# Three edits to an attention and mixture-of-experts kernel: batch 1's late values by split products, the first expert in five chunks, 512-column products in the last two second layers

## The chip, the cores and the metric

The kernel runs on one core of one Trainium2 chip. The metric is the device time of one execution in microseconds (us); the time of a kernel is the median of its timed runs. A profile of one more execution shows where each engine's time goes.

## The reference

An attention over channels feeds a mixture of experts. Cut to what matters:

```python
# attention: B, N, C = 4, 5056, 256
qn = q / (norm(q, axis=1) + 1e-6);  kn = k / (norm(k, axis=1) + 1e-6)
a = softmax(kn.T @ qn / tau)            # 256 x 256 for each batch
x = (v @ a).reshape(20224, 256)         # the "values"
# experts: E = 8, F = 1024, cap = 20224 / 8 = 2528
logits = x @ w_gate
# all (token, expert) pairs in order of falling logit: a token goes to the first
# expert that still has room; each expert ends with 2528 tokens
out[mask_e] = relu(x[mask_e] @ w1[e]) @ w2[e]
```

## The kernel before

**Values.** Each batch has five chunks (b, c) of 1024 rows, the last one padded, and a chunk has eight tiles of 128 rows (t). A tile of values is v times a, a contraction over 256 channels in two halves (kb). It can be made in two ways. `x_tiles` (L260) multiplies in plain float32: two matmuls of 256 columns, which the trace shows as four. `x_tiles_cut` (L572) works with float32r numbers: v and a are each held as a high and a low half, and a tile takes six matmuls of 256 columns: high·high, high·low and low·high for each kb. This is called a tile by three products. `cleave` (L559) makes the halves of half a chunk (four tiles): ScalarE writes minus the high half, an accumulating DMA issued by GpSimd adds v from DRAM to it, which leaves the low half, and ScalarE writes the high half. Batch 0 is made by three products while the scores are still being computed (L306), batch 2 by `x_tiles_cut`, batches 1 and 3 in plain float32.

**Routing.** When all logits are there, `route` (L615) finds each expert's members one expert after another: eight rounds each of a VectorE comparison (`ge`, L728), a TensorE count (`pc`, L693), small VectorE reductions and a second small product (L706). Then `compact` and `listed` write the list of the expert's rows (`src`, L1014). For expert 0 the list comes in two parts: the first four columns of 128 rows (`HEAD` = 4, taken from the rows stored so far) and the other sixteen. The routing of expert p + 1 runs while expert p is computed.

**The order around the change.** The tail of the values is an order written out by hand: `TURNS` is a string of F and C. F makes half a chunk of the `PLAIN` list (two pairs of tiles) in plain float32, C half a chunk of the `CLOVEN` list by three products. Meanwhile VectorE routes expert 0. After the last turn the kernel waits, in its planned time, for the first list; then it makes the last eight pairs of tiles (`LATE` = 8), which are batch 3's chunks 3 and 4. In front of the last of these pairs `turn_both` transposes chunk 0 of expert 0, which has two columns. A planner (`Order`, L1106) holds estimated clocks of TensorE (`o.pe`) and VectorE (`o.dve`). While the main work is written down, it places the routing's steps in each engine's order when the planned clock has passed their readiness. The engines themselves keep that order and wait on semaphores.

**Experts.** An expert's 20 columns are cut into chunks: `FIRST_CUT` = 2, 4, 4, 4, 4, 2 for expert 0, `CUT` = 4, 4, 4, 4, 4 for the others. `load_x` gathers the rows of a chunk by one indirect DMA for each column. They are transposed by TensorE (`turn`, L1423; the first three chunks of expert 0 and chunks that are in a hurry) or by VectorE and DMAs (`stage`), and split into `xH` and `xL`. `layer1` (L1480) makes eight blocks `ph` of 128 hidden units with six products each; ScalarE writes `hH`, VectorE `hL`. `layer2` (L1523) makes for each column a `py` of 256 outputs in 24 products: for each of eight blocks hH·wH, hH·wL and hL·wH. ScalarE copies `py` to `y`, and GpSimd scatters the rows. Layers of neighbouring chunks are interleaved: layer 1 of chunk c, then layer 2 of chunk c − 1. `split_piece` (L1244) splits the weights in quarters. For expert 0, what of them is not split by the start of its first layer is split right there, before it.

Of the kernel before, what the change touches and what calls it, by code (L numbers as in the profile page):

```python
# [8 lines left out]
F32 = mybir.dt.float32  # L9
# [60 lines left out]
PLAIN = ((3, 0), (1, 2), (3, 1), (3, 2), (1, 3), (1, 4), (3, 3), (3, 4))  # L70
CLOVEN = ((2, 4), (2, 0), (2, 1), (2, 2), (2, 3))
TURNS = "FFCFCFCFCFCFCFCFCFFCFC"
PLACES = ("ub0", "ub1", "ua0", "ua1", "ub0", "ub1", "vr", "ua0", "ua1", "ua2")
BEHIND = {3: "FF", 4: "C", 5: "CC", 6: "FFFF", 7: "CCC", 8: "CCCC", 9: "FFFFFF"}
FREED = (9, 10)
CUT = (4, 4, 4, 4, 4)
FIRST_CUT = (2, 4, 4, 4, 4, 2)
# [21 lines left out]
DEPTH = 3  # L99
WOVEN = range(1, E - 1)  # L100
# [4 lines left out]
def attention_moe(ctx: ExitStack, tc: tile.TileContext, q, k, vt, tau, wg, w1t, w2t, tabs, out):  # L105
# [21 lines left out]
    ps_2 = Banks("s0", "s1")  # L127
# [428 lines left out]
    cloven = [(b, c, h) for b, c in CLOVEN for h in range(0, T, TH)]  # L556
    v_cut = []

    def cleave():  # L559
        b, c, h = cloven[len(v_cut)]  # L560
        home = PLACES[len(v_cut)]
        y = (vp.tile([128, 2048], F32, name="vr", bufs=BUFS_V) if home == "vr" else
             ffw.tile([128, 2048], F32, name=home)).bitcast(F32R)
        y = y.rearrange("p (z k n) -> p z k n", z=2, k=2)
        raw = vs[b, c][:, :, h:h + TH].rearrange("p k t n -> p k (t n)")
        S.activation(y[:, 1], raw, AF.Copy, scale=-1.0)
        P.dma_start(out=y[:, 1], in_=vt[b, c].rearrange("p (k n) -> p k n", k=2)[:, :, h * 128:(h + TH) * 128],
                    accum_op=OP.add)
        S.activation(y[:, 0], raw, AF.Copy)
        v_cut.append(y.rearrange("p z k (t n) -> p z k t n", t=TH))  # L570

    def x_tiles_cut(k, t, xs, tick):  # L572
        b = cloven[k][0]
# [640 lines left out]
    cuts = [FIRST_CUT] + [CUT] * (E - 1)  # L1214
# [28 lines left out]

    def split_piece(p, i, q_, eng):  # L1244
# [6 lines left out]
        if i == 1:  # L1251
# [49 lines left out]
    phs = []  # L1301
    turned = [0]
# [154 lines left out]
    def turn_both():  # L1457
        xg = xgs[0, 0]
        ready[0, 0] = 2
        nt = n_of(0, 0)  # L1460
        xH, xL = xts[0, 0] = (ffx.tile([128, 2, 512], F32R, name="xH"), ffx.tile([128, 2, 512], F32R, name="xL"))
        pt = ps_t.tile([128, 512], F32, name="pt")
        for i in range(cuts[0][0]):
            for kb in range(2):
                PE.transpose(pt[:, kb * nt + i * 128:kb * nt + (i + 1) * 128].bitcast(F32R),
                             xg[:, i, kb * 128:(kb + 1) * 128].bitcast(F32R), identr)
        for kb in range(2):
            rows, hi = even_odd(pt[:, kb * nt:(kb + 1) * nt]), in_turn(xH, kb, nt)
            S.activation(hi, rows, AF.Copy)
            V.tensor_tensor(in_turn(xL, kb, nt), rows, hi.bitcast(F32), op=OP.subtract)  # L1470
        o.pe += 450
        o.dve = max(o.dve, o.pe + 1200)

# [49 lines left out]
    def layer2(p, c, h, inserts):  # L1523
# [4 lines left out]
        wH, wL = wt[p, 1]  # L1528
        o.until(("out", p))
        settle()  # L1530
        pace_2 = 2 if p < 2 else 3
        for i, col in enumerate(cols_of(p, c)):
# [5 lines left out]
            py = ps_2.tile([128, 512], F32, name="py")  # L1538
            j = 0
            for fb in range(8):  # L1540
                for l, w in ((hH, wH), (hH, wL), (hL, wH)):
                    w = w.rearrange("p (g a f m) -> p g f m a", g=4, a=2, f=2)[:, fb // 2, fb % 2]
                    PE.matmul(py[:n, 0:C], lhsT=l[:, fb, tk], rhs=w, start=(j == 0), stop=(j == 23))  # L1543
                    j += 1
                    if j == 12:
                        for fn in inserts.get((i, j), ()):
                            fn()
                        advance(2, i * 2688 + 1344, (2, p, c))
                    if j % pace_2 == 0:
                        o.tick(pace_2 * 112)  # L1550
            y = ffx.tile([128, C], F32, name="y", bufs=4)
            S.activation(y[:n], py[:n, 0:C], AF.Copy)  # L1552
            P.memset(spacer[:, 0:1], 0.0)
# [226 lines left out]
```

## Time and profile before

| | |
|---|---|
| timed runs | 1222.14, 1218.46, 1221.15 us; median 1221.15 us |
| the profiled execution | 1213.0 us, of which the span is 1211.1 us |
| TensorE busy | 1195.4 us (99%) |
| VectorE busy | 863.6 us (71%) |
| ScalarE busy | 580.8 us (48%) |
| GpSimd busy | 407.8 us (34%) |
| mean granted clock of TensorE | 0.999 |

The span is the time from the first to the last event of the profile; the execution's own time is a little longer. The busy times of one engine never overlap with themselves, so an engine at 99% leaves 1% of the span in which it did nothing. Shares are means over stages that differ.

### The profile page before, as it was taken

How to read it: one execution, taken by the hardware profiler on the slowest of the kernel's cores; microseconds unless marked ns; L12 is line 12 of the kernel's file. 1: busy time of each engine (PE TensorE's matmuls, PEld its weight loads, DVE VectorE, ACT ScalarE, POOL GpSimd, SP SyncE). 2: the span in 40 equal slices, each digit the busy share in tenths (PEclk: the TensorE clock that was granted, in tenths of full speed). 3: DMA queues.
4: the chain of work that ended last, by engine and by line, in shares of the span. 5: the costliest groups of instructions: out<-in, count | busy, mean ns of one | idle time of the engine just before them, and what ended most of it. 6: DMA issues, size and time to landing. Idle time of an engine off the chain costs nothing.

```text
span 1211.1 us, 23720 instructions
## 1 busy us (share of the span) xinstructions
PE 1195.4 (99%) x8885; PEld 1095.1 (90%) x8885; DVE 863.6 (71%) x2428; ACT 580.8 (48%) x1326; POOL 407.8 (34%) x655
## 2 busy tenths in 40 slices
PE   8999999999999999999999999999999999999997
PEld 6889977898998989899999999999999999999997
DVE  7788695778888888988887888887764444435330
ACT  6566654656434453444353464364465544344331
POOL 1000001111442552354425443443444345444422
PEclk9999999999999999999999999999999999999999
DMA  8999986785333132323422242243234233422310
GB/s 313 362 397 318 405 323 209 182 232 225 113 105 122 59 103 79 124 75 99 152 88 75 90 157 97 84 162 99 88 130 136 87 117 126 147 92 95 105 65 34
DMA packets 70546, 183.82 MB, mean 152 GB/s; under 512 B 11168, under 2 KB 34592, under 8 KB 65824
## 3 DMA queue, kind: packets, MB, share of 16 engines
q1 hardware_dynamic: 39808, 97.01, 22.3%
q0 software_dynamic: 20656, 63.72, 17.5%
q10 hardware_dynamic: 9968, 21.59, 4.7%
q8 instruction: 69, 1.13, 0.4%
q14 instruction: 45, 0.37, 0.1%
HBM read 122.77 MB, written 59.24 MB: 150 GB/s over the span
## 4 chain that ended last, share of the span: by engine, by line
PE 88%; DVE 4%; issue 4%; POOL 2%; DMA 1%; ACT 0%; POOLq 0%; SPq 0%; ACTq 0%; DVEq 0%
PE ph L1506 32%; PE py L1543 31%; PE s L343 9%; PE px L265 5%; PE pc L693 2%; PE px L306 2%; PE px L581 2%; PE px L459 1%; POOL out_dram L1554 1%; DMA ua<-in_q_dram 1%; DVE acc_k L353 1%; DVE acc_q L353 1%; PE pi L933 1%; PE pt L933 0%; DVE nf L410 0%
## 5 line engine op out<-in xcount | busy, mean ns | idle before, releaser
L1543 PE MATMUL py<-ua,hH 128*128 128x256 f32 (+1 forms) x2560 | 438.4, 277 | 0.0
L1506 PE MATMUL ph<-xH,ua 128*128 128x512 f32 (+3 forms) x1312 | 393.4, 375 | 0.3 <-DVE hL L1515 0.3
L1543 PEld LDWEIGHTS py<-ua,hH 128*128 128x128 f32 (+1 forms) x2560 | 389.3, 190 | 1.7
L1543 PE MATMUL py<-ua,hL 128*128 128x256 f32 (+1 forms) x1280 | 352.8, 276 | 0.0
L1515 DVE SCALAR_TENSOR_TENSOR hL<-ph,hH 128x512 fp32r<-128x512 f32 (+3 forms) x328 | 217.6, 666 | 111.1 <-ACT hH L1510 110.3
L1510 ACT ACTIVATE hH<-ph 128x512 fp32r<-128x512 f32 (+3 forms) x328 | 191.0, 583 | 198.2 <-PE ph L1506 196.8
L1506 PEld LDWEIGHTS ph<-xH,ua 128*128 128x128 f32 x1312 | 244.6, 189 | 30.1 <-DVE hL L1515 1.4
L1554 POOL DMA_INDIRECT out_dram<-y,idx x160 | 162.3, 1015 | 292.8 <-ACT y L1552 239.1
L1506 PE MATMUL ph<-xL,ua 128*128 128x512 f32 (+3 forms) x656 | 245.1, 374 | 0.0
L1543 PEld LDWEIGHTS py<-ua,hL 128*128 128x128 f32 (+1 forms) x1280 | 243.9, 191 | 0.0
L1276 POOL DMA_INDIRECT xg<-x_d,src x160 | 164.6, 1029 | 90.7 <-issue 51.5
L1552 ACT ACTIVATE y<-py 128x256 f32<-128x256 f32 (+1 forms) x160 | 61.5, 384 | 259.1 <-PE py L1543 199.9
L343 PE MATMUL s<-ua 128*128 128x256 f32 (+1 forms) x640 | 144.8, 385 | 5.7 <-DMA ua<-in_q_dram 5.7
L343 PEld LDWEIGHTS s<-ua 128*128 128x128 f32 (+1 forms) x640 | 121.7, 193 | 25.4 <-DMA ua<-in_q_dram 5.7
L1506 PEld LDWEIGHTS ph<-xL,ua 128*128 128x128 f32 x656 | 124.2, 189 | 13.9 <-DVE xL L1448 0.8
L352 ACT ACTIVATE sq<-ua 128x1024 f32<-128x1024 f32 (+1 forms) x80 | 76.8, 970 | 49.5 <-DVE acc_k L353 15.4
L1374 DVE TENSOR_TENSOR xL<-xT,xH 128x256 fp32r<-128x256 f32 (+1 forms) x136 | 50.3, 419 | 59.1 <-ACT xH L1370 59.0
L1287 POOL COPY spacer<-hH 1x1 f32<-1x1 f32 x110 | 25.9, 235 | 154.4 <-ACT hH L1510 144.7
L373 POOL TENSOR_SCALAR ny<-ny 128x4 f32<-128x4 f32 x4 | 2.0, 504 | 179.6 <-ACT ny L372 179.6
L1257 DVE TENSOR_TENSOR ua<-ub,ua 128x512 fp32r<-128x512 f32 x64 | 47.1, 745 | 14.8 <-ACT ua L1254 13.8
L1370 ACT ACTIVATE xH<-xT 128x256 fp32r<-128x256 f32 (+1 forms) x136 | 52.2, 448 | 2.6 <-DMA xT<-via 2.6
L353 DVE TENSOR_TENSOR acc_k<-acc_k,sq 128x1024 f32<-128x1024 f32 (+2 forms) x40 | 44.2, 1112 | 10.4 <-ACT sq L352 9.5
(346 smaller groups left out, 1419.8 us busy)
## 6 DMA issues: line engine op xcount, KB each, us to landing
x_d<-xs ACTq DMA_DIRECT2D x40, 512.0 KB, 5.4
ua<-in_k_dram SPq DMA_DIRECT2D x35, 512.0 KB, 6.5
ua<-in_q_dram SPq DMA_DIRECT2D x35, 512.0 KB, 7.5
via<-xs SPq DMA_DIRECT2D x33, 512.0 KB, 2.7
xT<-via SPq DMA_DIRECT2D x132, 128.0 KB, 2.8
vr<-in_vt_dram SPq DMA_DIRECT2D x14, 1024.0 KB, 10.3
ua<-in_vt_dram SPq DMA_DIRECT2D x4, 1024.0 KB, 4.8
ua<-in_vt_dram POOLq DMA_DIRECT2D x5, 512.0 KB
```

Of the source, the lines that this page charges most:

```text
L265: mm = PE.matmul(px[:, i * C:i * C + width], lhsT=vs[b, c][:, kb, t + i, :], rhs=a_f[b][:, kb, 0:width], start=(kb == 0), stop=(kb == 1))
L343: newest[0] = PE.matmul(sb[:, ib * C:(ib + 1) * C], lhsT=kt[:np_, t, ib * 128:(ib + 1) * 128], rhs=qt[:np_, t, :], start=(first and t == 0 ...
L352: S.activation(sq[:n, t0:t1], t_[:n, t0:t1], AF.Square)
L353: V.tensor_tensor(acc[:n, t0:t1], acc[:n, t0:t1], sq[:n, t0:t1], op=OP.add)
L1276: P.indirect_dma_start(out=xg[:n, i, :], out_offset=None, in_=rows, in_offset=bass.IndirectOffsetOnAxis(ap=routed[p]["src", col][:n, col:c ...
L1370: S.activation(hi[:, a], rows[:, a], AF.Copy)
L1506: PE.matmul(ph[:, 0:nt], lhsT=l[:, w], rhs=in_turn(x_, kb, nt).rearrange("p a m -> p m a"), start=(i == 0), stop=(i == 5))
L1510: S.activation(hH[:, fb, 0:nt], ph[:, 0:nt], AF.Relu)
L1515: V.scalar_tensor_tensor(hL[:, fb, 0:nt], ph[:, 0:nt], 0.0, hH[:, fb, 0:nt].bitcast(F32), op0=OP.max, op1=OP.subtract)
L1543: PE.matmul(py[:n, 0:C], lhsT=l[:, fb, tk], rhs=w, start=(j == 0), stop=(j == 23))
L1552: S.activation(y[:n], py[:n, 0:C], AF.Copy)
L1554: sd = P.indirect_dma_start(out=out, out_offset=bass.IndirectOffsetOnAxis(ap=routed[p]["idx", col][:n, col:col + 1], axis=0), in_=y[:n], i ...
```

## The change

1. Batch 1's chunks 2, 3 and 4 move from `PLAIN` to `CLOVEN`: six half chunks that were F become C. Their low halves come from a VectorE subtraction (v minus its high half), not from a DMA; a's halves for batch 1 are made by `halve_a_1`. `TURNS` has six F and sixteen C instead of twelve and ten. One more buffer, `own`, holds halves.
2. Expert 0 is cut like the others, in five chunks of four columns. Its first chunk is gathered in front of the last but one late pair and transposed by `turn`, one half in front of each of the last two pairs. Pieces of the weights left over are split between the blocks of its first layer. The second layer of a first chunk waits for the first part of the list alone.
3. In experts 6 and 7 (`WIDE` = 6) w2's halves lie side by side, and hH·wH and hH·wL become one product of 512 columns into the two halves of a PSUM bank. ScalarE copies the second half, VectorE adds the first, and four banks take turns. The last column of the last expert stays as it was.

```diff
+PLAIN = ((3, 0), (3, 1), (3, 2), (3, 3), (3, 4))
+CLOVEN = ((2, 4, 0), (1, 2, 0), (2, 4, 4), (1, 2, 4), (2, 0, 0), (1, 3, 0), (2, 0, 4), (1, 3, 4), (2, 1, 0), (1, 4, 0), (2, 1, 4),
+          (1, 4, 4), (2, 2, 0), (2, 2, 4), (2, 3, 0), (2, 3, 4))
-TURNS = "FFCFCFCFCFCFCFCFCFFCFC"
+TURNS = "FFCCCCFCCCCFCCCCFCCFCC"
+PLACES = ("ub0", "ub1", "own", "ua0") * 3 + ("vr", "vr", "vr", "own")
-FIRST_CUT = (2, 4, 4, 4, 4, 2)
+SUM_LAT = 700
+WIDE = 6
...
+    def halve_a_1():
+        a = a_f[1][:, :, 0:C].rearrange("p k (m a) -> p k m a", a=2)
+        less = x_rows()[:, 0:2].rearrange("p k (m a) -> p k m a", a=2)
+        h = apart(apool.tile([128, 2, GW], F32R, name="a0"))[:, :, :, 0:128]
+        S.activation(h.rearrange("p a k m -> p k m a"), a, AF.Copy)
+        V.tensor_tensor(less, a, h.rearrange("p a k m -> p k m a").bitcast(F32), op=OP.subtract)
+        lo = apart(apool.tile([128, 2, GW], F32R, name="a1"))[:, :, :, 0:128]
+        S.activation(lo.rearrange("p a k m -> p k m a"), less, AF.Copy)
...
+        if b == 2:
+            S.activation(y[:, 1], raw, AF.Copy, scale=-1.0)
+            P.dma_start(out=y[:, 1], in_=vt[b, c].rearrange("p (k n) -> p k n", k=2)[:, :, h * 128:(h + TH) * 128],
+                        accum_op=OP.add)
+            S.activation(y[:, 0], raw, AF.Copy)
+        else:
+            S.activation(y[:, 0], raw, AF.Copy)
+            unit[0] += 1
+            o.post(o.pe + TURN_LAT, 1120,
+                   lambda: V.tensor_tensor(y[:, 1], raw, y[:, 0].bitcast(F32), op=OP.subtract), unit[0])
+            lows_of[len(v_cut)] = unit[0]
...
+    cuts = [CUT] * E
...
-        o.until(("out", p))
+        o.until(("out", p, 0) if c == 0 else ("out", p))
...
+                todo = [(one, hH, wH), (one, hH, wL), (one, hL, wH)]
+                if twice:
+                    todo = [(py[:n], hH, w.rearrange("p a z m -> p (z m) a")), (one, hL, wH)]
...
-            S.activation(y[:n], py[:n, 0:C], AF.Copy)
+            S.activation(y[:n], py[:n, C:2 * C] if twice else one, AF.Copy)
+
+            def store(py=py, y=y, col=col, n=n, twice=twice):
+                if twice:
+                    V.tensor_tensor(y[:n], py[:n, 0:C], y[:n], op=OP.add)
...
-            if n == LATE - 1:
+            if n == LATE - 2:
                 queue[:] = head[:HEAD]
                 while queue:
                     gather()
-                turn_both()
+            if n >= LATE - 2:
+                turn(0, 0, n - LATE + 2)
             pair(*at_)
...
-        for i, q_, eng in cut_w[0][1:]:
-            split_piece(0, i, q_, eng)
...
-                h[0] = layer1(p, 0, {} if p == 0 else {2: [turn_at(1, 0)], 7: [turn_at(1, 1)], **pieces})
+                left_w = {2 * at: [lambda x=x: split_piece(0, *x)] for at, x in enumerate(cut_w[0][1:])}
+                h[0] = layer1(p, 0, left_w if p == 0 else {2: [turn_at(1, 0)], 7: [turn_at(1, 1)], **pieces})
...
-                    layer2(p, 0, h[0], {1: [turn_at(1, 0)], (1, 12): [turn_at(1, 1)]})
+                    layer2(p, 0, h[0], {3: [turn_at(1, 0)], (3, 12): [turn_at(1, 1)]})
```

## Rows read from the trace of the kernel before

**Rows 1.** The page: the span, then busy time, share and instructions of each engine.

```profile
span 1211.1 us, 23720 instructions
PE 1195.4 (99%) x8885; PEld 1095.1 (90%) x8885; DVE 863.6 (71%) x2428; ACT 580.8 (48%) x1326; POOL 407.8 (34%) x655
```

**Rows 2.** Windows: from:to, length, each engine's busy time (instructions), granted clock, DMA.

```profile
240.00:255.00 15.00, 15.00 (x149) 14.02 (x148) 12.13 (x39) 11.69 (x19) 3.26 (x3) 1.00 1.03 257
311.00:424.00 113.00, 112.39 (x958) 105.06 (x956) 96.02 (x312) 46.67 (x122) 48.35 (x75) 1.00 0.28 93
988.00:1100.00 112.00, 112.00 (x758) 105.27 (x757) 50.05 (x85) 46.32 (x94) 49.90 (x84) 1.00 0.38 123
```

**Rows 3.** The chain of waits in order of time: start, us, what.

```profile
225.20 2.68 PE px L581 x24
227.88 3.46 PE px L265 x16
...
984.60 10.36 PE ph L1506 x48
994.96 10.66 PE py L1543 x96
...
1015.98 10.72 PE py L1543 x96
```

**Rows 4.** Timeline of TensorE: start, us, operation, count, idle before it.

```profile
287.15 0.16 PE L913 MATMUL pc<-cb,before 128*128 128x1 bf16 x1 [0.67 <-DVE cb L907]
...
307.96 0.64 PE L1465 MATMUL pt<-identr,xg 128*128 128x128 f32 x4
...
330.01 0.28 PE L1442 MATMUL pt<-identr,xg 128*128 128x128 f32 x1 [0.31 <-DMA xg<-x_d,src]
...
432.59 0.45 PE L1442 MATMUL pt<-identr,xg 128*128 128x128 f32 x4
...
521.92 0.47 PE L1442 MATMUL pt<-identr,xg 128*128 128x128 f32 x4
```

**Rows 5.** Groups by line: busy us, mean ns of one, idle before.

```profile
L353 DVE TENSOR_TENSOR acc_k<-acc_k,sq 128x1024 f32<-128x1024 f32 (+2 forms) x40 | 44.2, 1112 | 10.4 <-ACT sq L352 9.5 <-ACT acc_k L348 0.5
...
L569 ACT ACTIVATE ua<-vr 128x1024 fp32r<-128x1024 f32 x5 | 5.2, 1040 | 0.0
```

**Rows 6.** Timeline of VectorE: expert 0's routing, and one addition of 256 columns.

```profile
219.28 0.82 DVE L609 TENSOR_TENSOR eq<-L 128x640 f32<-128x640 f32 x1
...
284.49 0.17 DVE L1014 COPY_PREDICATED src<-early,w__2663 128x4 int32<-128x4 int32 x1
...
306.53 0.18 DVE L1014 COPY_PREDICATED src<-early,w__2783 128x16 int32<-128x16 int32 x1
...
310.12 0.42 DVE L1470 TENSOR_TENSOR xL<-pt,xH 128x256 fp32r<-128x256 f32 x1 [0.45 <-ACT xH L1469]
```

**Rows 7.** DMA issues by line: count, KB each, median us from issue to landing.

```profile
xg<-x_d,src POOLq DMA_INDIRECT x160, 2.8
...
ub<-in_vt_dram POOLq DMA_DIRECT2D x4, 512.0 KB, 8.3
```

**Rows 8.** Timelines of ScalarE's queue and GpSimd: last store, gathers of three chunks.

```profile
297.19 0.33 ACTq L275 DMA_DIRECT2D x_d<-xs  x1
...
300.80 0.95 POOL L1276 DMA_INDIRECT xg<-x_d,src  x1 [20.90 <-ACT xs L269]
...
305.09 0.94 POOL L1276 DMA_INDIRECT xg<-x_d,src  x1 [0.30 <-issue]
...
424.70 0.97 POOL L1276 DMA_INDIRECT xg<-x_d,src  x1 [0.30 <-issue]
...
515.70 0.98 POOL L1276 DMA_INDIRECT xg<-x_d,src  x1 [0.16 <-issue]
```

**Rows 9.** List columns written (L1014), experts 1 and 2: count, durations, first and last start.

```profile
L1014 DVE COPY_PREDICATED src<-early,w__4187 x2: 170/174/179, 396.3 to 412.2; 128x6 int32<-128x6 int32 x1, 128x14 int32<-128x14 int32 x1
L1014 DVE COPY_PREDICATED src<-early,w__5817 x2: 171/175/179, 502.6 to 515.4; 128x6 int32<-128x6 int32 x1, 128x14 int32<-128x14 int32 x1
```

More of the change, by code (lines that the diff above doesn't have):

```diff
@@ L1250, in split_piece @@
         raw, h, lo = raw[:, sl], h[:, sl], lo[:, sl]
-        if i == 1:
+        if i == 1 and p >= WIDE:
+            raw = raw.rearrange("p (f m a) -> p f a m", f=2, a=2)
+            h, lo = (blocks(p, q_ * 2)[:, q_ % 2 * 2:q_ % 2 * 2 + 2, :, z] for z in range(2))
+        elif i == 1:
             raw = raw.rearrange("p (m a) -> p a m", a=2)
@@ L1455, in turn @@
             load_ahead(p, c)
[L1457 to L1472, printed above, removed]
     def load_ahead(p, c):
@@ L1544, in layer2 @@
                     j += 1
-                    if j == 12:
-                        for fn in inserts.get((i, j), ()):
+                    if fb == 3 and at_end:
+                        for fn in inserts.get((i, 12), ()):
                             fn()
                         advance(2, i * 2688 + 1344, (2, p, c))
-                    if j % pace_2 == 0:
+                    if twice:
+                        o.tick(218 if to is not one else 110)
+                    elif j % pace_2 == 0:
@@ L1550, in layer2 @@
                         o.tick(pace_2 * 112)
             y = ffx.tile([128, C], F32, name="y", bufs=4)
-            S.activation(y[:n], py[:n, 0:C], AF.Copy)
-            P.memset(spacer[:, 0:1], 0.0)
-            sd = P.indirect_dma_start(out=out, out_offset=bass.IndirectOffsetOnAxis(
-                ap=routed[p]["idx", col][:n, col:col + 1], axis=0),
-                                      in_=y[:n], in_offset=None)
-            for s_ in scat:
-                tc.declare_no_dep(sd.ins, s_.ins, reason="each token is written once")
@@ L1559, in layer2 @@
-            scat.append(sd)
+            S.activation(y[:n], py[:n, C:2 * C] if twice else one, AF.Copy)
+            def store(py=py, y=y, col=col, n=n, twice=twice):
+                if twice:
+                    V.tensor_tensor(y[:n], py[:n, 0:C], y[:n], op=OP.add)
+                P.memset(spacer[:, 0:1], 0.0)
+                sd = P.indirect_dma_start(out=out, out_offset=bass.IndirectOffsetOnAxis(
+                    ap=routed[p]["idx", col][:n, col:col + 1], axis=0),
+                                          in_=y[:n], in_offset=None)
+                for s_ in scat:
+                    tc.declare_no_dep(sd.ins, s_.ins, reason="each token is written once")
+                scat.append(sd)
@@ L1560, in layer2 @@
+            if twice:
+                unit[0] += 1
+                pys.append(unit[0])
+                o.post(o.pe + SUM_LAT, 400, store, unit[0])
+            else:
+                if p >= WIDE:
+                    o.flush(unit[0])
+                store()
             settle()
@@ L1570, in first_w @@
         def first_w():
+            assert past.count("C") >= 10
             load_w(0, 0)
@@ L1597, in attention_moe @@
         place()
+        halve_a_1()
         P.memset(ge[:, :, NT:J], 0.0)
         for kind in TURNS:
-            while len(v_cut) < len(cloven) and len(v_cut) <= len(past) + 1:
-                want_ = BEHIND.get(len(v_cut), "")
-                if any(past.count(x) < want_.count(x) for x in set(want_)):
-                    break
+            while len(v_cut) < len(CLOVEN) and len(v_cut) <= len(past) + 1 and len(v_cut) < past.count("C") + 4:
                 cleave()
@@ L1620, in attention_moe @@
         actx.close()
+        cctx.close()
         px_at[1] = False
```

52 lines of the change are left out of this document (31 added, 21 removed).

## The prediction

> **What bounds the kernel now.** I read the page first: the span is 1211.1 us and TensorE is busy for 1195.4 of them, VectorE for 863.6 [rows 1]. So all but 15.7 us of the span is matmul time, and the first question for each edit is how much TensorE time it takes away. The windows come second, because the share is a mean: while expert 0 is routed between the values, TensorE has no gap and VectorE is busy for 12.13 of 15 us; while expert 0 is computed VectorE is busy for 96.02 of 113 us, and from 988 to 1100 us, in the last experts, for 50.05 of 112 [rows 2]. The granted clock is 1.00 in all of them, so the 2.4 GHz level holds and no price here is one of a slow clock. VectorE therefore has room at the end of the kernel and little in front of it, and the second question is whether its new work makes a routing list late. The chain of waits gives the prices of products without idle time in between [rows 3]; the timelines show how close the lists and gathers come to the products that need them [rows 4, 6, 8, 9].
>
> **The change part by part.** All sums are in microseconds against the profiled execution, 1213.0 us around its span of 1211.1. The median of the runs shown is 1221.15, so 8.15 are added at the end; the last execution's extra time is taken as common to both kernels.
>
> *Values of batch 1.* Half a chunk in plain float32 takes 3.46 (16 instructions), by three products 2.68 (24 instructions) [rows 3]. The difference is 0.78; six half chunks save 4.68. They cost ScalarE six writes of a high half at 1.040 each, 6.2 in all [rows 5], which is hidden: ScalarE is busy for 11.69 of 15 us in its densest window, the four PSUM buffers of the values let it lag by some products, and batch 2's ten DMA halves are now spread over a longer stretch. They cost VectorE six subtractions of 1024 elements a row, at 1.112 like the additions of that size [rows 5], and one of 512 for a; by half of that row about 0.6, together 7.3. This work stands in front of or inside expert 0's routing, which runs on VectorE from 219.28 to the first list at 284.49 [rows 6]. VectorE is idle for a fifth of this stretch, but in short waits for TensorE's counts, so I take 5.5 of the 7.3 as delay; the bounds are 0 (all in the gaps) and 7.3. What is late next: the first list at 290.0 in place of 284.5. It is needed by the first gather, at 300.80, and that gather starts 3.6 after the last store issued at 297.19 [rows 8], so it waits for the store and not for the list. In the new kernel the stores end some 4.7 us earlier, so the gather would start near 296: still 6 us behind the list. Cost nothing, with 1 at most if the planner's clock runs ahead while it waits for the list.
>
> *Low halves of batch 2.* The order CCCC instead of FCFC shortens the lead of an accumulating DMA. It needs 8.3 from issue to landing [rows 7]. It is issued about one and a half C after the C that frees its place, and used after two or three more C, one F and a routing count: 2.68 × 2.5 + 3.46 = 10.2 from issue. Margin about 2; the row gives a median and no spread, so I allow 0 to 2 of stall and take 0.3.
>
> *Expert 0 in five chunks.* Columns stay the same. One chunk of 512 columns replaces two of 256: 48 products at 10.36 / 48 = 0.2158 instead of 96 at 10.72 / 96 = 0.1117 [rows 3], 0.36 less. TensorE transposes the first three chunks, now twelve columns instead of ten: four transposes more, below 0.45 for four [rows 4]. The two cancel. The wait of 0.31 for a gather at 330.01 [rows 4] should go, since chunk 2 is now needed a whole layer later, and the 0.67 of waiting at 287.15 may go, as the second list's count moves behind it among the late pairs: I take 0.6 for both together, from 0 to 0.98. Against that, the first chunk's transposes now need four gathered columns, and in front of the last but one pair. From the first gather at 300.80 the fourth was issued at 305.09 and lands 2.8 later, at 307.9 [rows 7, 8]. The transposes stood at 307.96 [rows 4], seven pairs of 1.73 (half of 3.46) behind the last turn, which so ended near 295.9; the fourth column landed 12.0 after that. In the new order the transposes follow after six pairs, 10.4. So the wait is 1.6 at most, and less by the second list's counts, which now fall among the late pairs and hold up the pairs but not the gathers; I take 0.4, with 0 below. The splitting of leftover weights stands in front of nothing that TensorE needs at once.
>
> *Products of 512 columns.* Per block the old form takes three products at 0.1117, 0.335; the new one takes 0.2158 + 0.1117 = 0.3275. That is 0.0075 less, for 8 blocks × 39 columns (two experts of 20, less the last), 2.35 less. The nearest row is layer 1, which streams 512 columns in the same even-odd order at 0.2158 each, so the gain is between 0 (if the mix with 256 columns breaks the pace) and 2.35, and I take all of it. The page "TensorE: Matmul & The Clock Gate" of the Trainium skill gives, in its section "Back-to-back issue gap", N/2.4 + 2.5 ns for a warm matmul, which agrees at 512 columns but gives 109.2 where this trace has 111.7 at 256; by it the gain would be an estimated 0.78 instead of 2.35. The same section puts a sustained stream of 512-column products at about 131 ns; the trace's 215.8 does not agree. VectorE gets 39 additions of 256 columns at 0.42 [rows 6], 16.4 in all, hidden because it is idle for more than half of that stretch [rows 2]; if that cover were gone, each column would still have 2.6 for 0.42. The very last column keeps its old form, so the tail behind the last product stays.
>
> *Later lists.* TensorE arrives at expert 1 about 5.5 earlier, the routing about 3.5 later (5.5 less what expert 0 gives VectorE back: one chunk less that VectorE transposes and splits). Chunk 1 of expert 1 was gathered last at 424.70, landed 2.8 later at 427.5, and was transposed at 432.59: 5.1 to spare [rows 4, 7, 8]. Chunk 0 of expert 2 was gathered last at 515.70, landed at 518.5, transposed at 521.92: 3.4 to spare. The lists stood at 412.2 and 502.6 [rows 9], well before these gathers, and the gathers follow TensorE's own pace, so part of a delay is swallowed; the bounds are 0 and 9 − 5.1 + 9 − 3.4 = 9.5 for both; I take 1.0, near the lower end because a turn that isn't ready is put off behind the next column of layer 2.
>
> *Sum.* −4.68 (values) − 0.6 (old waits) − 2.35 (512 columns) + 0.3 (DMA lead) + 0.4 (first gathers) + 1.0 (later lists) = −5.9. The profile would come to 1207.1, the median to 1221.15 − 5.9 = **1215.2**.
>
> **The rivals.**
> *Half of it is eaten by waits.* The same savings of 7.6, but the lead of the DMAs costs its 2, the first gathers 1.6, and the later lists 1: the sum is −3.0, or 1218.1. For it: margins of about 2 and of nothing. Against it: all three at their dear end.
> *The lists decide; the kernel gets slower.* The place is the transposes at 432.59 and 521.92. If the routing keeps its whole delay of 7.3 and TensorE its lead of 6, the gathers there are 13.3 late against margins of 5.1 and 3.4: 8.2 + 9.9 = 18 if both are paid in full, about 12 if the planner puts half of the second off. Against 7.6 of savings this is +4.4, or 1225.5. It decides from about 7.6 of waits in all, that is, a shift of some 8 us against TensorE. For it: VectorE's 85% during expert 0 leaves little to catch up with. Against it: from expert 1's list to expert 2's 106.3 us pass [rows 9], and an expert's products alone take 105.4 (five layers of 10.36 and five of 10.72), to which the routing's counts are added, so the lag doesn't grow; and the gathers, which TensorE's progress releases, swallow a part.
> *The wide products bring nothing.* Then 2.35 is missing: 1217.6. For it: the excess over the columns, 5.0 ns at 256 and 2.5 at 512, is small, and no row has the two sizes in turn.
>
> **How the numbers follow.** Forecast 0.57, with its own range 1213 to 1217.5; half eaten 0.19; slower 0.11; wide products without gain 0.08; more than the sum (all waits gone) 0.05. A difference of 0.3%, 3.7 us, is about what a measurement of this kernel can tell from no change: 1217.5 is that border below. Faster: 0.57 + 0.05, half of the third rival and a little of the first, 0.68. Same: the rest of these and the mildest of the slower case, 0.22. Slower 0.10. The range runs from 1210.5 (the full 7.6 and 3 more for old waits that I have not seen and for the spread of the runs, which lie 3.7 apart) to 1221, which takes in the half-eaten case and leaves out the slower one.
>
> **What would show it.** Right: 96 instructions fewer at the plain products and 144 more by three products, no idle in front of either; `py` with 312 products of 512 columns, some 0.327 for a pair of them; a layer 2 of four columns in experts 6 and 7 of 10.48 instead of 10.72; the first list near 290 and the first gather near 296. Wrong: idle in front of products by three (the DMA lead), of the first transposes, or of the transposes of experts 1 and 2 (late lists). The prediction fails if the routing's delay is much over 5.5, or if TensorE's saved time turns up as waiting for a list.

## The result and the profile after

The changed kernel takes 1231.55 us (median, 1230.04 to 1234.58) against 1220.71 before on the same chip: a ratio of 1.0097, 95% interval 1.0083 to 1.0112. It is slower by 10.8 us between the medians (11.8 by the ratio); 1215.2 was forecast, and 1231.55 lies above the range, which ended at 1221. The profiled execution took 1234.58 around this span, with 292 instructions fewer on TensorE than in [rows 1] and 3.4 us more of busy time:

```profile
span 1232.8 us, 23148 instructions
PE 1198.8 (97%) x8593; PEld 1085.0 (88%) x8593; DVE 882.9 (72%) x2452; ACT 585.6 (47%) x1318; POOL 407.3 (33%) x652
```

The two spans differ by 21.7 us, twice as much as the medians: the profiled execution of the kernel before, 1213.0, was 8 us under its median. 5.5 of it lie ahead of the change: the first of the last values' pairs starts at 223.49 instead of 218.03, after code that is the same in both, and in the other kernels' profiles below it starts anywhere from 217.7 to 222.9. So stages are compared by their lengths:

| stage (us) | before | after |
|---|---|---|
| last values: first pair to first product of layer 1 | 92.7 | 100.9 |
| from there to expert 0's first layer 1 on ScalarE | 1.4 | 2.8 |
| experts 0 to 4, up to the same point of expert 5 | 565.6 | 575.0 |
| experts 5 to 7, to the end of the span | 333.4 | 330.6 |

The last row is the third part and came as forecast. In the chain of waits (start, us, what), a layer 2 of four columns takes 10.48 in experts 6 and 7, where it was 10.72 or 10.66 [rows 3]:

```profile
1019.38 10.66 PE py L1569 x96
1030.04 10.36 PE ph L1519 x48
1040.40 10.48 PE py L1569 x64
```

The first three rows are the loss, 8.2, 1.4 and 9.4. Not all of the 9.4 come with the change: wide_only, below, has the order of the kernel before in experts 0 to 4 and took 569.1 there, and own_fourth_turn has the changed kernel's and took 565.8. At the start of the values, ScalarE and then VectorE (timelines) stand still:

```profile
224.74 1.06 ACT L580 ACTIVATE own<-ua 128x1024 fp32r<-128x1024 f32 x1 [5.97 <-DVE L L465]
```

```profile
224.35 0.27 DVE L465 COPY L<-turned 128x128 f32<-128x128 f32 x1
228.87 0.70 DVE L562 TENSOR_TENSOR xs<-a,a 128x512 f32<-128x512 f32 x1 [4.25 <-ACT a L561]
229.49 1.22 DVE L588 TENSOR_TENSOR ub<-vr,ub 128x1024 fp32r<-128x1024 f32 x1
230.62 0.82 DVE L632 TENSOR_TENSOR eq<-L 128x640 f32<-128x640 f32 x1
...
302.54 0.17 DVE L1037 COPY_PREDICATED src<-early,w__2829 128x4 int32<-128x4 int32 x1
```

The new buffer `own` was opened when the score phase's pool had closed, and its first write waits for the last logits copy on VectorE (L465). Behind it in ScalarE's queue stand both batches' halves of a, and VectorE, in order, waits for the high half of a (L561) before it can begin the routing. So the routing starts 7.1 us after the first pair (1.25 before), and the first list comes 79.0 us after it (66.5 before, both from the first pair to the list [rows 6]): 12.6 later, not 5.5.

TensorE feels this long before a gather, because the routing's counts (L716) and second products (L729) stand in its own queue, between the turns. Windows from the first pair to the first late pair, before and after (length, then TensorE's busy time), and TensorE's waits in the second (sum, count, longest):

```profile
218.03:295.95 77.92, 77.17 (x627) 70.81 (x626) 65.08 (x227) 43.65 (x81) 9.90 (x10) 1.00 0.75 222
223.49:301.59 78.10, 72.87 (x658) 68.09 (x656) 60.78 (x186) 51.51 (x83) 12.10 (x12) 1.00 0.74 206
```

```profile
PE pc L716 <- DVE ge L751: 2.7, 5, 1.5
PE pc L729 <- DVE Ex L725: 1.1, 1, 1.1
PE pc L716 <- ACT eq L744: 0.8, 2, 0.5
PE px L604 <- ACT xs L270: 0.5, 1, 0.5
```

The turns got 4.3 us cheaper and end no earlier: TensorE waits the difference out. At the far end (GpSimd's gathers, ScalarE's queue, TensorE):

```profile
309.64 0.96 POOL L1305 DMA_INDIRECT xg<-x_d,src  x1 [12.31 <-DVE khi L663]
...
313.75 1.84 POOL L1305 DMA_INDIRECT xg<-x_d,src  x1 [0.30 <-issue]
```

```profile
302.42 0.33 ACTq L276 DMA_DIRECT2D x_d<-xs  x1
304.31 0.60 ACT L270 ACTIVATE xs<-px 128x512 f32<-128x512 f32 x1 [1.92 <-DMA x_d<-xs]
```

```profile
315.51 0.28 PE L1472 MATMUL pt<-identr,xg 128*128 128x128 f32 x1 [0.91 <-DMA xg<-x_d,src]
316.21 0.28 PE L1472 MATMUL pt<-identr,xg 128*128 128x128 f32 x1 [0.41 <-DMA xg<-x_d,src]
319.00 0.28 PE L1472 MATMUL pt<-identr,xg 128*128 128x128 f32 x1 [2.51 <-DMA xg<-x_d,src]
319.11 2.88 PE L266 MATMUL px<-a_last,vr 128*128 128x256 f32 x8
321.43 1.03 PE L1472 MATMUL pt<-identr,xg 128*128 128x128 f32 x4
322.25 2.53 PE L266 MATMUL px<-a_last,vr 128*128 128x256 f32 x8
```

```profile
PE pt L1472 <- DMA xg<-x_d,src: 3.8, 3, 2.5
```

The store of the last turn is issued 78.9 after the first pair (79.2 before), and the first gather starts 7.2 behind it, where it was 3.6 [rows 8]: 86.2 after the first pair, 82.8 before. TensorE waits 3.8 for its rows (the last row), the largest of its waits in this stage, and then the pair of eight takes 2.32 (319.11 to 321.43) instead of 1.73. The windows give the reason (granted clock: third number from the end):

```profile
314.30:319.00 4.70, 0.86 (x8) 0.44 (x5) 1.99 (x5) 1.16 (x2) 1.30 (x1) 1.00 0.59 179
319.00:324.40 5.40, 5.40 (x20) 4.50 (x21) 2.50 (x6) 3.72 (x13) 0.00 (x0) 0.68 0.00 0
```

After 4.7 us with 0.86 of work the granted clock is 0.68 for 5.4 us: part of it ran at 1.2 GHz. In the experts the same happens at a routing product (Ex). VectorE, which makes Ex, has stood for 4.80 ahead of it (first row, VectorE; the last section comes back to that), and behind the wait two products of 480 columns take 1.00 instead of 0.57, at a granted clock of 0.54 (last row, a window):

```profile
646.61 0.19 DVE L719 TENSOR_TENSOR Dm<-pc,dmask 128x32 f32<-128x32 f32 x1 [4.80 <-remote]
644.40 0.57 PE L1519 MATMUL ph<-xH,ua 128*128 128x480 f32 x2
647.36 0.30 PE L729 MATMUL pc<-Ex,ones_q 128*128 128x64 f32 x1 [2.39 <-DVE Ex L725]
...
647.87 1.00 PE L1519 MATMUL ph<-xH,ua 128*128 128x480 f32 x2
647.36:651.00 3.64, 3.64 (x10) 3.10 (x11) 3.09 (x10) 2.28 (x10) 0.00 (x0) 0.54 0.00 0
```

TensorE's waits in experts 0 to 4, in the view of waits, sum to 7.4 us (1.7 before):

```profile
PE pc L729 <- DVE Ex L725: 4.9, 3, 2.4
PE ph L1519 <- DVE hL L1528: 1.6, 3, 0.8
PE pc L716 <- DVE ge L751: 0.6, 2, 0.4
PE pt L956 <- PE pi L956: 0.3, 1, 0.3
```

### The profile page after: what moved, and what is told of

Its sections match the earlier page's. It is cut to its first block, busy times and chain, and to the rows that moved or that the text cites. A ratio compares the mean times of both kernels' runs of the same rounds, so it can differ in the third digit from the quotient of the medians.

```text
span 1232.8 us, 23148 instructions
## 1 busy us (share of the span) xinstructions
PE 1198.8 (97%) x8593; PEld 1085.0 (88%) x8593; DVE 882.9 (72%) x2452; ACT 585.6 (47%) x1318; POOL 407.3 (33%) x652
## 4 chain that ended last, share of the span: by engine, by line
PE 71%; DVE 13%; issue 5%; DMA 4%; ACT 3%; POOL 2%; another core or an unknown queue 0%; ACTq 0%; POOLq 0%; SPq 0%; DVEq 0%
PE py L1569 29%; PE ph L1519 28%; PE s L344 5%; PE pc L716 2%; PE px L266 2%; DMA ua<-in_k_dram 1%; DMA ua<-in_q_dram 1%; PE px L307 1%; DVE hL L1528 1%; POOL out_dram L1587 1%; DMA x_d<-xs 1%; DVE acc_k L354 1%; DVE acc_q L354 1%; DVE ge L751 1%; PE px L460 1%
## 5 line engine op out<-in xcount | busy, mean ns | idle before, releaser
L1569 PE MATMUL py<-ua,hH 128*128 128x256 f32 (+2 forms) x2248 | 436.0, 292 | 0.0
L1519 PE MATMUL ph<-xH,ua 128*128 128x512 f32 (+1 forms) x1280 | 392.9, 381 | 1.6 <-DVE hL L1528 1.6
L1569 PEld LDWEIGHTS py<-ua,hH 128*128 128x128 f32 (+1 forms) x2248 | 350.7, 190 | 7.8
L1569 PE MATMUL py<-ua,hL 128*128 128x256 f32 (+1 forms) x1280 | 345.6, 275 | 0.0
L1523 ACT ACTIVATE hH<-ph 128x512 fp32r<-128x512 f32 (+1 forms) x320 | 189.6, 593 | 194.7 <-PE ph L1519 182.9
L1528 DVE SCALAR_TENSOR_TENSOR hL<-ph,hH 128x512 fp32r<-128x512 f32 (+1 forms) x320 | 216.2, 678 | 78.6 <-ACT hH L1523 63.2
L1519 PE MATMUL ph<-xL,ua 128*128 128x512 f32 (+1 forms) x640 | 243.3, 380 | 0.1
L1519 PEld LDWEIGHTS ph<-xL,ua 128*128 128x128 f32 x640 | 121.5, 190 | 14.2 <-DVE xL L1478 0.7
L1316 POOL COPY spacer<-hH 1x1 f32<-1x1 f32 x107 | 22.5, 210 | 142.9 <-ACT hH L1523 140.9
L1404 DVE TENSOR_TENSOR xL<-xT,xH 128x256 fp32r<-128x256 f32 x124 | 47.3, 427 | 28.0 <-ACT xH L1400 27.9
L1585 DVE TENSOR_TENSOR y<-py,y 128x256 f32<-128x256 f32 (+1 forms) x39 | 16.6, 425 | 65.5 <-ACT y L1581 65.5
```

What stands on the lines that cost most here:

```text
L1404: V.tensor_tensor(lo[:, a], rows[:, a], hi[:, a].bitcast(F32), op=OP.subtract)
L1519: PE.matmul(ph[:, 0:nt], lhsT=l[:, w], rhs=in_turn(x_, kb, nt).rearrange("p a m -> p m a"), start=(i == 0), stop=(i == 5))
L1523: S.activation(hH[:, fb, 0:nt], ph[:, 0:nt], AF.Relu)
L1528: V.scalar_tensor_tensor(hL[:, fb, 0:nt], ph[:, 0:nt], 0.0, hH[:, fb, 0:nt].bitcast(F32), op0=OP.max, op1=OP.subtract)
L1569: PE.matmul(to, lhsT=l[:, fb, tk], rhs=r, start=(fb == 0 and k_ == 0), stop=(fb == 7 and at_end), skip_group_check=twice)
```

## The experiments

Ratios are to the kernel before on the same chip, with 95% intervals; 0.1% is 1.2 us.

The chips are not alike. The kernel before took 1214.5 to 1214.6 us on the chips of own_fourth_dma, own_fourth_late, own_fourth_turn, five_wide, fw_shift, no_low_tick and own_fourth_tick (here called group A), and 1219.8 to 1220.8 on those of the result and of all other runs (group B). A ratio takes this out only where both kernels lose alike. Three pairs of kernels have the same instructions in the same order on TensorE, VectorE, ScalarE and GpSimd in experts 0 to 4, and their profiles there show (us, and TensorE's waits in it):

| pair (A, B) | on A | on B |
|---|---|---|
| five_wide, five_only | 562.4, waits 1.4 | 572.7, waits 7.3 |
| own_fourth_late, after_late | 564.9, waits 1.5 | 574.2, waits 7.6 |
| own_fourth_dma, no_low | 566.5, waits 2.7 | 578.4, waits 9.4 |

VectorE's longest idle time in experts 0 to 4 is 1.5 to 1.9 us in the seven profiles of A and in that of the kernel before, and 3.1 to 5.5 us in the twelve of B, the changed kernel's among them. So the tables above compare a profile like A's with one of B. Each is one execution; five_only's was its slowest, 4.1 over its median. As the medians of the kernel before lie some 6 us apart, an estimate from the last pair (11.9 less 6.2) is that up to 0.5% between ratios of A and B can come from the chips. So ratios are compared within a group, and a comparison across the two is marked.

**Which part.** The hunks of each part alone in the kernel before, and those of the last two together. The list's time, here and below, is the start of its tests (the first G, L946; L923 before): 61.4 after the first pair before, 73.5 in the changed kernel, 71.4 in own_fourth.

> The kernel before with the third part alone (512-column products in the second layers of the last two experts). Both theories: expert 6 and expert 7 together 2 to 3 us shorter, everything ahead of expert 6 unchanged, so 1218 us against 1220.7 before (ratio 0.9978). If it is no faster, the gain of 2.7 us that the two experts show in the changed kernel has another cause.

0.9970 [0.9959, 0.9981]: a gain of 3.7 us.

> The kernel before with the second part alone (first expert in five chunks, its first gather and transposes two pairs ahead of the end of the values). Theory (the loss comes from batch 1's values): within 2 us of before, 1219 to 1222.5 us. Rival (the earlier gather and the transposes of chunk 0 stall TensorE): 4 to 8 us slower than before, 1225 to 1229 us, with one wait of over 2 us at the transposes of the first chunk.

0.9995 [0.9984, 1.0007]: as the theory.

> The kernel before with the first part alone (batch 1's late values by three products, low halves by VectorE). Theory: this part carries the loss, 7 to 12 us slower than before, 1228 to 1233 us; ScalarE stands 6 us at the third cleave's copy and the first list is some 10 us later than before. Rival (the part saves its 4.7 us and the loss is in the chunks): 1216 to 1220 us.

1.0227 [1.0204, 1.0251], over twice the theory. Beside a first chunk of two columns, TensorE also waits 7.0 for gathers at the transposes of expert 0's next chunks.

> The kernel before with the second and the third part, without the first (batch 1's values stay fp32). Theory that the parts add (wide products alone 0.9970, five chunks alone 0.9995) and the first part carries the loss: 0.9965 of before, 1215 to 1217 us. Rival (the first part only pays or costs beside the chunks, or the chunks cost with the wide products): 1219 us or more.

0.9969 [0.9959, 0.9979]. Parts two and three add up (wide_only and five_only, both B, make 0.9965), and beside them the first part costs 1.0097 - 0.9969 = 1.28%, 15.6 us (1.32% from the sum on B), where it was to save 4.4.

**ScalarE's wait for the buffer.**

```diff
-CLOVEN = ((2, 4, 0), (1, 2, 0), (2, 4, 4), (1, 2, 4), ...
-PLACES = ("ub0", "ub1", "own", "ua0") * 3 + ...
+CLOVEN = ((2, 4, 0), (2, 4, 4), (1, 2, 0), (1, 2, 4), ...
+PLACES = ("ub0", "ub1", "ua0", "own") * 3 + ...
```

> The changed kernel with the third half chunk cleaved into ua0 and the fourth into the new buffer, so that ScalarE's first write into the new buffer comes two fp32 pairs-of-pairs later, when the buffers of the score phase under it are long free. Theory that the wait of 6 us of ScalarE for that space is the main loss: 4 to 6 us faster than the changed kernel, 1225.5 to 1227.5 us. Rival (the low halves on VectorE and the moved routing are the main loss): at most 1.5 us faster, 1230 to 1231.5 us.

1.0059 [1.0040, 1.0079]. The wait of 5.97 is gone, and the routing starts 2.5 after the first pair; 0.38% (4.6 us, both on B, intervals apart) belong to it. The rest stays.

**What else the first part costs.** The low halves later, by DMA and by GpSimd; then the transposes' place.

```diff
-            o.post(o.pe + TURN_LAT, 1120, ...subtract...)
+            o.post(o.pe + 4500, 1230, ...subtract...)
```

> The kernel own_fourth with each of the six subtractions due 3350 ns later in the planner's order and costed at 1230 ns instead of 1120, so that they stand behind routing steps until the high half is written. Theory: VectorE's waits for ScalarE of some 4 us go, the first list comes 3 to 5 us earlier than in own_fourth, and the time falls 3 to 5 us, to 1221 to 1223 us. Rival (the 7 us of the subtractions themselves, wherever they stand): within 1.5 us of own_fourth, 1224.5 to 1227.5 us.

1.0008 [0.9999, 1.0016], 0.5% better, but across the groups (A against own_fourth's B). The list comes at 67.4, and the turns end 72.5 after the first pair (76.2 in own_fourth).

> The changed kernel with the six subtractions due 3350 ns later and costed at 1230 ns, and the new buffer where the change has it. Theory that the two mends add (the buffer 0.4%, the subtractions 0.5% of before): 1.004 to 1.006 of before. Rival (ScalarE's wait for the buffer only hurts because subtractions stand in VectorE's queue behind it): 1.000 to 1.002.

1.0078 [1.0058, 1.0098]: with the buffer where the change has it, the same edit gives 0.2%, within B. Neither theory's number. That the two mends do not add isn't shown: this kernel and own_fourth_late are the second pair of the table, 574.2 and 564.9 in experts 0 to 4 with one order.

```diff
-        if b == 2:
+        if b > 0:
             S.activation(y[:, 1], raw, AF.Copy, scale=-1.0)
```

> The kernel own_fourth with batch 1's low halves made as batch 2's are (negative copy, accumulating DMA, high copy): VectorE's six subtractions and its waits for ScalarE's high halves are gone, ScalarE and GpSimd's queue do six more half copies and six more DMAs. Theory (the subtractions in VectorE's queue delay the first list, and TensorE's routing products and first gathers wait for it): first list back within 3 us of before, so 8 us earlier than in own_fourth, and the time 5 to 9 us below own_fourth's 1226.1, 1217 to 1221 us. Rival (the earlier transposes and the chunks cost it): within 2 us of own_fourth, 1224 to 1227 us.

1.0045 [1.0028, 1.0063]. The theory's 5 us did not come, although the list is 6.4 earlier than in own_fourth: the stage still takes 98.8 (own_fourth 99.0). The 0.14% between the two are across the groups and show nothing.

```diff
-            o.post(o.pe + TURN_LAT, 1120, ...subtract...)
+            P.tensor_tensor(y[:, 1], raw, y[:, 0].bitcast(F32), op=OP.subtract)
```

> The kernel own_fourth with batch 1's low halves subtracted by GpSimd instead of VectorE: no subtraction in the routing's queue and no added DMA. Theory (VectorE's share and its waits delay the list, and the saving of 4.7 us on TensorE is real): first list within 2 us of before, 5 us or more faster than own_fourth, ratio to before 0.995 to 1.0015. Rival (TensorE waits for the stores and gathers whatever VectorE does, or GpSimd's subtractions are long and stand ahead of batch 2's DMAs): ratio 1.003 to 1.008.

1.0101 [1.0083, 1.0119], the rival and worse. One subtraction takes GpSimd 2.4 us (1.22 on VectorE).

```diff
-            if n == LATE - 2:
+            if n == LATE - 1:
...
-            if n >= LATE - 2:
-                turn(0, 0, n - LATE + 2)
+                turn(0, 0, 0)
+                turn(0, 0, 1)
```

> The kernel own_fourth with the first gathers and both transposes of chunk 0 one pair later, ahead of the last pair as in the kernel before. Theory (the list is late, so the gathered rows are late wherever the transposes stand): the waits at the transposes of 0.8 and 3.0 us shrink by the pair of 1.7 us that now runs ahead of them and come back in part behind the last pair, 0 to 2 us faster, 1224 to 1226 us. Rival (the place of the transposes is the main loss): 4 us or more faster, below 1222.5 us.

1.0036 [1.0025, 1.0047], a little over the theory against own_fourth, but across the groups: this kernel has own_fourth's order in experts 0 to 4, and they take 565.8 on A and 572.1 on B. So it isn't shown that the place gives the 0.23%.

> The kernel own_fourth with both mends: the subtractions due later, as in own_fourth_late (1.0008 of before), and the first gathers and transposes one pair later, as in own_fourth_turn (0.9977 of own_fourth). If the two add: 0.9985 of before. If the transposes' wait was already met by the earlier list of own_fourth_late: 1.0005 to 1.0015. No theory here gives less than five_wide's 0.9969.

1.0157 [1.0136, 1.0178]: no theory had it. The stage is the shortest of these kernels, 92.5, but expert 0 takes 130.5 us instead of own_fourth_late's 116.6 (across the groups, but more than they differ), with waits of 4.1 for gathers (three, the longest 2.4) and of 2.34 for VectorE's low half at one chunk's transposes, and a mean granted clock of 0.93.

> The kernel five_wide with the first gathers and both transposes of chunk 0 one pair later, ahead of the last pair. Theory (with a list in time, the place moves a wait of 1.1 us behind a pair of 1.7 us): 0.9955 to 0.9975 of before. Rival (transposes ahead of the last pair hold up the gathers of the next chunks, as in late_turn): 1.003 or more, with waits of over 2 us at the transposes of the later chunks of the first expert.

1.0038 [1.0022, 1.0053], the rival's number: the place alone costs 0.7%, against five_wide and against the sum 0.9965 on its own group. Not the rival's mechanism: in expert 0, which takes 123.9, no transposes wait for a gather, but routing products wait 3.5 for Ex. Such waits do not need the place: five_only, on B with five_wide's order, waits 4.7 for Ex in experts 0 to 4, and its expert 0 takes 121.5 (five_wide, on A, 116.3).

**Single costs, put into five_wide.**

```diff
+        if len(v_cut) in (1, 3, 4, 5, 6, 7):
+            o.post(o.pe + TURN_LAT, 1120, ...own[:, 0:1024] = L - L...)
```

> The kernel five_wide with six subtractions of 1024 fp32 elements added to VectorE in the routing of the first expert, due as the changed kernel's are, reading the logits and writing a buffer that nobody reads: the cost of VectorE's share without ScalarE, TensorE or any DMA behind it. Theory (VectorE's 7 us move the first list and every later one): first list 6 to 8 us later, 3 to 7 us slower than five_wide, ratio to before 0.9995 to 1.0025. Rival (VectorE has the room): within 1.2 us of five_wide, ratio 0.996 to 0.998.

1.0037 [1.0023, 1.0050]: six subtractions that nobody reads cost 0.68%, 8.3 us, more than their own length (0.72% against the sum on B). The list is 4.6 later, at 66.0, less than the theory. Most is paid in experts 0 to 4: 576.3 with 7.5 us of waits, where fw_load, below and on the same chip, takes 564.6. But the edit also moves the planner's clock, and the routing stands elsewhere among the products there; which of the two is paid, the run can't tell.

```diff
-        want(("ei", 0), first_w)
+        want(("ei", 0), lambda: w_at.__setitem__(0, o.pe + 8000))
+            if w_at[0] and o.pe >= w_at[0] and not cut_w[0]: first_w()
```

> The kernel five_wide (fp32 values of batch 1, five chunks, wide products) with the load of the first expert's weights (two DMAs of 1 MB) issued 8 us later in the planner's order, where the changed kernel issues them, so that it runs beside the last stores of the values instead of ahead of them. Theory (the stores that the first gathers wait for land in some 6 us instead of 2.9 because of it): first gather 3 to 4 us later than in five_wide's 82.8 us after the first pair, 2 to 5 us slower than five_wide, ratio to before 0.9985 to 1.001. Rival (the stores' landing is not what the gathers wait for): within 1 us of five_wide, ratio 0.996 to 0.9977.

0.9952 [0.9933, 0.9972], the rival's number, but the theory was not put to the test: the load was issued at 279.27, 59.5 after the first pair, just as in five_wide. In the changed kernel it is issued 71.5 after the first pair, and the stores behind it land late; whether one makes the other stays untried.

**The saving and the order.** First without the low halves:

```diff
-            o.post(...subtract...)
-                vH, vL = (v_cut[k][:, z, kb, t + i] for z in range(2))
+                vH, vL = (v_cut[k][:, z if b == 2 else 0, kb, t + i] for z in range(2))
```

> The kernel own_fourth without batch 1's low halves: they are not computed, and TensorE's third product reads the high half in their place, so its work is that of the change and VectorE has no subtraction. Theory (VectorE's share is what eats the first part): first list within 2 us of five_wide's 61.4 us after the first pair, ratio to before 0.993 (all of TensorE's 4.7 us arrives, from five_wide's 0.9969) to 0.9972 (none of it arrives, the gathers set the end of the stage). Rival (ScalarE's copies, the later weight load or the DMAs of the cloven halves cost as much): 1.000 or more.

1.0067 [1.0048, 1.0087], the rival's: no subtractions, a list in time (61.6), and still 1% behind five_wide (across the groups). The stage takes 95.8 (five_wide 94.6): the turns end 3.6 earlier, 74.5 after the first pair, but then TensorE waits 3.5 for gathers (five_wide 1.1), at a mean granted clock of 0.96 in the stage (1.00). And experts 0 to 4 take 578.4 for the same products, with 9.4 us of waits. The next theory was the order in which the planner put the routing among the products. The order can't be all of it: own_fourth_dma has the same one there and takes 566.5. The planner's clock of TensorE does not hold the wait at the gathers:

```diff
+            if n == LATE - 2:
+                for _ in range(60):
+                    o.tick(100)
```

> The kernel no_low (no low halves for batch 1, the high half read in their place) with 6 us added to the planner's clock of TensorE ahead of the first transposes, about what TensorE waits there for the gathers. Theory (order by a clock that is off): the waits and slow products of experts 0 to 4 fall from 32 us towards five_wide's 18 us, ratio to before 0.995 to 1.001. Rival: no change from no_low's 1.0067, 1.004 or more.

0.9981 [0.9970, 0.9991], as the theory, but from B to A: the 0.86% against no_low are order and chip together. Windows of expert 2 (length, then TensorE's busy time), without and with the edit, and TensorE's waits in experts 0 to 4:

```profile
545.70:666.10 120.40, 117.52 (x963) 108.25 (x962) 96.91 (x302) 52.82 (x143) 46.38 (x71) 0.99 0.29 94
```

```profile
536.10:651.00 114.90, 114.67 (x958) 106.58 (x958) 97.38 (x312) 53.32 (x147) 50.81 (x81) 1.00 0.34 110
```

```profile
PE pc L725 <- DVE Ex L721: 6.1, 6, 2.4
PE ph L1515 <- DVE hL L1524: 2.1, 5, 0.7
```

```profile
PE pt L1468 <- DVE low L790: 0.7, 1, 0.7
PE pc L712 <- DVE ge L747: 0.5, 2, 0.3
```

The waits for Ex are gone; in own_fourth_dma, which has the first order on A, they are 0.3. Within A the mended order gains 4.5 us in experts 0 to 4 (562.0 against 566.5). The stage is unchanged at 95.8; TensorE (timeline) still stands at the transposes:

```profile
302.84 0.41 PE L1468 MATMUL pt<-identr,xg 128*128 128x128 f32 x1
304.64 0.62 PE L1468 MATMUL pt<-identr,xg 128*128 128x128 f32 x2 [1.39 <-DMA xg<-x_d,src]
307.18 0.28 PE L1468 MATMUL pt<-identr,xg 128*128 128x128 f32 x1 [1.92 <-DMA xg<-x_d,src]
```

> The kernel own_fourth, whole in its computation, with the same 6 us added to the planner's clock. Theory: 4 to 7 us faster than own_fourth's 1.0059, so 1.000 to 1.003 of before. Rival: 1.0045 or more.

1.0023 [1.0013, 1.0032], as the theory, with the whole computation: experts 0 to 4 take 562.7 with 1.1 us of waits. The 572.1 of own_fourth is from B; on A its order takes 565.8 (own_fourth_turn).

```diff
+        o.pe -= 4700
```

> The kernel five_wide with the planner's clock of TensorE set back by 4.7 us after the last of the turns, as if the first part had saved them: the same instructions, only the order of routing among products changes. Theory (the order, placed by a clock that is off, costs the time in the experts): 0.3% to 1% slower than five_wide's 0.9969, so 1.000 to 1.007 of before, with waits of TensorE for Ex of over 2 us in sum in experts 1 to 3. Rival (the order does not matter, the first part's own work costs): 0.996 to 0.998.

1.0015 [1.0002, 1.0028]. The order costs 0.46% with the work unchanged and within A, as the theory; but not where it said. There is no wait for Ex; the stage takes 98.2 instead of 94.6, with a wait of 2.37 at the first transposes, and experts 0 to 4 take 566.1 instead of 562.4.

## Why the prediction was wrong

The cost falls apart along five kernels, each one step from the next:

| kernel | ratio, group | step |
|---|---|---|
| five_wide | 0.9969, A | parts two and three alone |
| no_low_tick | 0.9981, A | + 0.12%: TensorE's products of the first part, order mended |
| own_fourth_tick | 1.0023, A | + 0.42% (5.1 us): VectorE's subtractions, on one chip |
| own_fourth | 1.0059, B | + 0.36% (4.4 us): the order without the mend, and the change of group |
| changed kernel | 1.0097, B | + 0.38% (4.6 us): the buffer's first write |

The third and the fifth row are measured within a group and clear of noise. How the fourth divides between order and chip is not shown.

*Values of batch 1, -4.68.* The first failed step. The products did get cheaper, but the saving did not arrive. In the changed kernel TensorE already waited it out between the turns, for the routing (72.87 busy instead of 77.17, in 78.10 instead of 77.92). And no_low_tick, without any of VectorE's subtractions, is 0.12% above five_wide, within noise, not 0.39% below. There the turns do end 3.6 earlier, and what ends last is the gather of the first rows: TensorE is at the transposes by 302.84 and waits for rows until 307.18. The text had the gather start 4.7 earlier because "the stores end some 4.7 us earlier"; even there it started 80.2 after the first pair, 2.6 earlier. In the changed kernel the last store was issued only 0.2 earlier, the gather started 7.2 and not 3.6 behind it, and so it came 3.4 later.

*"Cost nothing, with 1 at most if the planner's clock runs ahead".* The step that turned the sign. The routing's delay was followed only along the list to the first gather, and read as hidden behind the store. But TensorE itself has the routing's products in its queue: it waited 5.1 us for VectorE and ScalarE in the turns, where [rows 4] have 0.67. The list's delay was 12.6 and not 5.5: a subtraction takes 1.22 and not 1.112, the ones in the routing wait for ScalarE's high halves (2.09 and 1.54 in own_fourth), and the buffer's wait of 5.97 stood in no term at all. Behind the first gather the subtractions cost little by themselves: own_fourth_tick, which has them, takes 562.7 in experts 0 to 4, no_low_tick 562.0 on the same chip. Their 0.42% lie in the last values, 99.2 against 95.8.

*The planner's clock.* Named in half a sentence at 1 us; fw_shift measures it at 0.46% within A. The steps from own_fourth to own_fourth_tick (0.36%) and from no_low to no_low_tick (0.86%) hold the change of group too; within A, experts 0 to 4 show 3.1 and 4.5 us of them.

*Later lists, +1.0, and the rival "the lists decide".* The rival had the right sign, but its place, the transposes of experts 1 and 2, and its size, +4.4, were off: in the changed kernel no transposes there wait for a gather, and the waits in the experts are at routing products (Ex) and at low halves (hL).

*Old waits -0.6, first gathers +0.4.* Together five_only, 0.9995: right in sum as near as it can be measured, but not by its terms. The first gathers' wait was 1.1 there, and the old wait of 0.67 stayed (0.7). In the changed kernel the first gathers' wait is 3.8, above the bound of 1.6, as the first gather comes 3.4 later and not earlier.

*DMA lead +0.3.* No product by three waits for a low half's DMA in the changed kernel; in own_fourth_dma one does, for 1.85.

*The 8.15 between profile and median* were taken as common to both kernels. They weren't: the changed kernel's profiled execution is its slowest, 3.0 over its median.

*Products of 512 columns, -2.35.* Right: 10.48 for a layer 2, as forecast, and 0.9970 alone. The mix keeps its pace. By the Trainium skill's "TensorE: Matmul & The Clock Gate", section "Back-to-back issue gap", the estimate was 0.78; 3.7 (2.3 to 5.0) was measured, so the trace's own prices were the ones to use.

## What to carry to other kernels

A saving on the busiest engine counts only if that engine is what ends last at the next point where it needs data; follow the list, the store and the gather to that point before booking it. When an order is planned against a clock, a wait that the clock does not hold can cost twice, where it stands and in the steps placed after it (fw_shift: 0.46% by order alone); put measured waits into the clock when they change. Routing products in TensorE's queue tie it to VectorE: a delay of VectorE is not hidden because its last result is needed late. And measure two kernels on the same chip before explaining a few tenths of a per cent: one order took 566.5 and 578.4. A new buffer has an address: look at what used the space before, and at everything queued behind its first write.

The best of these is five_wide, or fw_load at 0.9952 with an overlapping interval: the second and third parts without the first.

## What the hardware showed unexpectedly

A wait costs more than its length. In five_wide TensorE waited 1.10 at the first transposes, and the granted clock stayed at 1.00:

```profile
307.40:309.00 1.60, 0.51 (x4) 0.28 (x2) 1.50 (x10) 0.60 (x1) 0.00 (x0) 1.00 0.60 164
309.00:313.80 4.80, 4.74 (x42) 4.07 (x43) 3.06 (x9) 1.68 (x3) 0.00 (x0) 1.00 0.28 113
```

In the changed kernel it waited 3.8 in three pieces, and the next 5.4 us ran at 0.68. By the order of the three buffers, a store of the values issued at 296.58 released its buffer only at 304.3 (the ScalarE row above), 7.7 later; in the last values before, the median from issue to landing was 2.7. Which other transfers slowed it was not settled.

Open stays a stall. In the changed kernel VectorE stands until 646.61 and ScalarE until 646.72 for products that TensorE issued by 643.3, and the releaser is named only as remote. VectorE's instruction behind it (Dm, L719) reads a count of the routing. In the pairs of one order the same instruction waits 4.82 in no_low and 1.38 in own_fourth_dma, 3.94 in five_only and 0.91 in five_wide, and in the changed kernel 4.13, 2.46 and 4.80 at three places where it waits 1.55, 1.21 and 1.37 in own_fourth_turn. From five_only, without the first part (VectorE, then ScalarE):

```profile
657.75 0.19 DVE L696 TENSOR_TENSOR Dm<-pc,dmask 128x32 f32<-128x32 f32 x1 [3.94 <-PE ph L1506]
657.86 0.60 ACT L1510 ACTIVATE hH<-ph 128x512 fp32r<-128x512 f32 x1 [3.86 <-PE ph L1506]
```

So these waits come with the chips of group B and need neither the first part nor its order. What differs on those chips is not known. Open also is why transposes one pair later hurt five_wide (0.7%) and, across the groups, own_fourth_late (1.5%).
